# One PSUM tile for each accumulator, the inner values' sums moved to GpSimd and partly through DRAM, splits of 1024 columns on VectorE

## The chip, the cores and the metric

The kernel runs on one core of a Trainium2 chip. The metric is the device time of one execution in microseconds; the median of three runs is compared. The profile is of one further execution, so it has a time of its own.

## The reference

Three layers follow each other on 4608 tokens of 512 values:

```python
# attention in chunks of 64: 8 batches, 8 heads, 576 positions, head size 64
attn = softmax(q @ k.T / sqrt(64)); x = attn @ v          # x: (4608, 512) after heads are joined
# first layer: w_in (512, 2048), w_out (2048, 512)
h = x @ w_in
x = (h * clip(h + 3, 0, 6) / 6) @ w_out
# second layer: w_in2 (512, 1024), w_out2 (1024, 512), g_ln (1024)
h = x @ w_in2
solu = h * softmax(h)
out = ((solu - mean) / sqrt(var + 1e-6) * g_ln) @ w_out2
```

All is float32. Each factor of a product is split into a rounded part and a rest (`hi`, `lo`), and a product is three matmuls: hi x hi, lo x hi, hi x lo.

## The kernel before, in words

The tokens are nine blocks of 512 columns, and attention has 36 units of 128 tokens, four to a block. A manual order of instructions is written out: each engine runs its own in the order of the code. Every wait is put in by the framework between instructions that touch the same tile.

Blocks 0 to 2 run the first layer plainly (`moe_h`, `moe_gate`, `moe_split`, `moe_o`), one chunk of 128 of the 2048 hidden values at a time, with the attention of later blocks between them; during blocks 1 and 2 the kernel also forms sums of weights (`sums_of`, `split_sums`) and stores them in DRAM. The blocks 3 to 8 are done as three pairs. A pair is two blocks that are treated as a matrix of 2 x 2 parts, so that seven products do instead of eight; the seven factors on either side are sums such as S1, S2 of weights and T1, T2 of inputs. The first two pairs run `pair_7`, the last one `pair`, beside which the class `Second` prepares the weights of the second layer. Then the second layer runs to the end.

`pair_7` has two halves.

- First half: eight steps j over pairs of hidden chunks. A step has seven products `mul7` of six matmuls each into accumulators a, b and c. In order of TensorE: A11 into a (ScalarE copies it to s1); S2 into b (VectorE: u2 = s1 + b); S1 into c; then, in `finish`, the last two products of the step before, A22 into its b and S4 into its c; S3 into b (VectorE: u3 = s1 + b, c22 = u3 + c); A12 into a; at last `att_slot`, the scores of one attention unit and the product with v of another. Steps 0 and 5 have no unit. Each of the four hidden values (c11 from a, c21 from b, c12 and c22 from c) goes through the gate h * clip(h / 6 + 1/2, 0, 1). `ring_tile` gives the weights of a step two buffers each: wa (A11, A12, A22) and ws (S1 to S4); `fetch_next(j + 2, ...)` loads them, from the SP queue, when `finish` has used the old ones.
- Second half: seven products i of eight chunks j each (`mul_o`, six matmuls a chunk), whose inputs are sums of the gated values. `prepare` splits one chunk and then, for the first four products, forms in place the sum that a later product needs. Six chunks are prepared ahead. Steps of `prep(p + 1)` (the inputs of the next pair) and two attention units stand between.

In the first half a and b are the halves of one tile of two PSUM banks, `acc_psum(j % 2)`, and the four values go to SBUF tiles `g_t` before their gates, two of them with the product on GpSimd (`gate_there`, L1214). `moe_o` takes its four accumulators from the same two tiles. At the end of the second pair `load_o` (L1398) loads 16 tiles of 512 KB of weights for the last pair: 8 in the last product, 8 behind it. Scores of units from 20 on go through `attn_scores` (VectorE subtracts the maximum, one exponential on ScalarE, VectorE sums), those before through `attn_scores_act` (eight exponentials of one head each, with the maximum as bias and the sum as a second output).

A tile of 128 x 512 float32 is 256 KB, one of 128 x 2 x 512 is 512 KB.

Of the kernel before, what the change touches and what calls it, by code (L numbers as in the profile page):

```python
# [8 lines left out]
F32 = mybir.dt.float32  # L9
# [7 lines left out]
P = 128  # L17
# [4 lines left out]
def tile_kernel(  # L22
# [33 lines left out]
    held = nc.dram_tensor("held", (NF, P, BT), F32, kind="Internal").ap()  # L56

# [50 lines left out]
    ps_acc = es.enter_context(tc.tile_pool(name="ps_acc", bufs=1, space=PSUM))  # L108
# [580 lines left out]
    rescale("i", 2)  # L689
    x2, xr2 = {}, {}  # L690
# [293 lines left out]
    def att_slot(w, u):  # L984
# [15 lines left out]
    def soft(u):  # L1000
        if u in exps:
            attn_exp_act(u, range(H))
        attn_norm(u)
# [186 lines left out]
    N_C, AHEAD = len(OUTS) * NJ, 6  # L1190
# [14 lines left out]
    def gate(h, out):  # L1205
        t = gp.tile([P, BT], F32, tag="t", name="t")
        nc.scalar.activation(out=t, in_=h, func=AF.Relu, bias=half_1, scale=1.0 / 6.0)
        nc.vector.scalar_tensor_tensor(out=out, in0=t, scalar=1.0, in1=h, op0=ALU.min, op1=ALU.mult)

    def gate_there(h):  # L1210
        t = gp.tile([P, BT], F32, tag="t", name="t")
        nc.scalar.activation(out=t, in_=h, func=AF.Relu, bias=half_1, scale=-1.0 / 6.0)
        nc.scalar.activation(out=t, in_=t, func=AF.Relu, bias=one_1, scale=-1.0)  # L1213
        nc.gpsimd.tensor_mul(out=h, in0=t, in1=h)  # L1214

    def source(c):
        i, j = divmod(c, NJ)
        f, h = ((0, 0), (1, 1), (1, 0), (1, 1), (0, 0), (0, 1), (1, 0))[i]
        return g_t[2 * j + f][:, h]

    def entry(c):
        if c < 5 * NJ:
            return pair_of(wi_slot(4 + c % 10, F32R))
        k = c % 6
        if k < 4:
            return pair_of(wi_slot(10 + k, F32R))
        return [gp.tile([P, BT], F32R, tag=n, name=n) for n in ("g_hi", "g_lo")]
# [3 lines left out]
    def prepare(c):  # L1231
        if c >= N_C:
            return
        i, j = divmod(c, NJ)
        src = source(c)
        hi, lo = parts_o[c] = entry(c)
        nc.scalar.copy(out=hi, in_=src)  # L1237
        (nc.vector if j % 4 == 3 else nc.gpsimd).tensor_sub(out=lo, in0=src, in1=hi.bitcast(F32))  # L1238
        (b11, b12), (b21, b22) = (pair_of(g_t[2 * j + f]) for f in range(2))
        if i < 4:  # L1240
            o, x, y = ((b11, b12, b11), (b12, b22, b12), (b22, b22, b11), (b21, b21, b22))[i]
            nc.vector.tensor_sub(out=o, in0=x, in1=y)

    def mul_o(ps, i, j, start, stop):
        w, x = ring_o[i, j // (NJ // 2)][:, j % (NJ // 2)], parts_o.pop(i * NJ + j)
# [11 lines left out]
    def pair_7(p, todo):  # L1257
        b1, b2 = FIRST + 2 * p, FIRST + 2 * p + 1
        base = (b1 + 2) * UPB
        late = None  # L1260

        def finish(j, b, c, s1, u2):
            mul7(b, j, "A22", "T4", False, True)
            fetch_next(j + 2, 0)
            c21, c12 = g_t[2 * j + 1][:, 0], g_t[2 * j][:, 1]
            nc.vector.tensor_add(out=c21, in0=s1, in1=b)
            gate(c21, c21)
            mul7(c, j, "S4", "B22", False, True)
            fetch_next(j + 2, 1)
            nc.vector.tensor_add(out=c12, in0=u2, in1=c)  # L1270
            gate_there(c12)
            ring_w.pop(j)

        event = {1: 0, 2: 1, 3: 2, 4: 3, 6: 4, 7: 5}
        for j in range(NJ):
            u = base + event[j] if j in event else NU
            m = acc_psum(j % 2) if j else att_psum()
            a, b = m[:, 0], m[:, 1]
# [5 lines left out]
            if u < NU and u != NA:  # L1284
                soft(u)
# [3 lines left out]
            if u < NU and u != NA:  # L1289
                attn_turn(u, range(3))  # L1290
            c = h_psum()
            mul7(c, j, "S1", "T1", True, False)
            for f in range(2):
                g_t[2 * j + f] = wo_slot(2 * j + f, F32)
# [456 lines left out]
```

## Time and profile before

| | us |
|---|---|
| median of 3 runs | 1352.29 |
| lowest and highest | 1345.01, 1353.33 |
| profiled execution | 1355.62 |
| its span, first to last instruction | 1353.8 |

| engine | busy us | share of the span | instructions |
|---|---|---|---|
| TensorE, matmuls (PE) | 1211.1 | 89% | 7199 |
| TensorE, weight loads (PEld) | 975.7 | 72% | 7199 |
| VectorE (DVE) | 967.7 | 71% | 1474 |
| ScalarE (ACT) | 713.0 | 53% | 1481 |
| GpSimd (POOL) | 538.5 | 40% | 586 |

The mean granted clock of TensorE is 0.957. Matmuls are pipelined and a matmul's end is modelled, so the busy time of TensorE is longer than the time that its matmuls take from start to start. A share of the whole span is a mean over stages that have different limits; the stages have to be looked at one by one. SPq is the queue from which SyncE issues DMAs.

### The profile page before, as it was taken

To read this page: it belongs to the slowest core of one execution; us is meant where nothing else is said; L and a number is where in the kernel's file an instruction comes from. 1 tells how busy PE (TensorE), PEld (TensorE's weight loads), DVE (VectorE), ACT (ScalarE), POOL (GpSimd) and SP (SyncE) were. 2 spreads that over 40 slices of the span, in tenths; PEclk is the share of its full clock that TensorE was granted. 3 is DMA by queue.
4 is the path that set the end of the run, shared out by engine and by line. 5 is a ranking of instruction groups with operands and counts; after the bars stand their busy time and mean duration, and the time that the engine had idled before them with its cause. 6 is when DMAs were issued, how large, how long until landed. Compare 5 with 4: busy or idle time off the path is not lost. (4 is left out here: it accounts for less than half of the span.)

```text
span 1353.8 us, 20715 instructions
## 1 busy us (share of the span) xinstructions
PE 1211.1 (89%) x7199; PEld 975.7 (72%) x7199; DVE 967.7 (71%) x1474; ACT 713.0 (53%) x1481; POOL 538.5 (40%) x586
## 2 busy tenths in 40 slices
PE   8999979998778678977857967999999999999998
PEld 6888757786556457755645856888888888888887
DVE  7986656774655689665569854667698887877874
ACT  7874444543333424433343422435488777777775
POOL 1003553410311448511154731211037767667665
PEclk9999999999988879999887988999999999999999
DMA  9715789622553545544442689978522222222221
GB/s 374 288 48 192 284 310 323 207 71 76 177 176 132 179 140 171 187 156 156 143 172 90 219 296 347 346 288 317 191 94 91 70 93 92 69 92 93 71 76 62
DMA packets 131225, 235.49 MB, mean 174 GB/s; under 512 B 15408, under 2 KB 75056, under 8 KB 124464
## 3 DMA queue, kind: packets, MB, share of 16 engines
q1 hardware_dynamic: 125936, 224.72, 48.6%
q10 hardware_dynamic: 5184, 9.44, 1.8%
q8 instruction: 57, 0.93, 0.3%
q14 instruction: 48, 0.39, 0.1%
HBM read 157.81 MB, written 65.54 MB: 165 GB/s over the span
## 5 line engine op out<-in xcount | busy, mean ns | idle before, releaser
L573 PE MATMUL acc<-g_hi,wo 128*128 128x512 f32 x640 | 164.1, 396 | 0.8 <-ACT g_hi L556 0.5
L1214 POOL TENSOR_TENSOR wo<-t,wo 128x512 f32<-128x512 f32 x32 | 41.1, 1285 | 258.9 <-ACT t L1213 164.8
L1238 POOL TENSOR_TENSOR wi<-wo,wi 128x512 fp32r<-128x512 f32 x74 | 119.4, 1642 | 52.7 <-ACT wi L1237 51.9
L573 PEld LDWEIGHTS acc<-g_hi,wo 128*128 128x128 f32 x640 | 119.5, 189 | 27.4 <-DVE xo L586 1.1
L1112 PE MATMUL hp<-wi,ws 128*128 128x512 f32 x384 | 103.5, 411 | 9.5 <-DVE s L1425 9.5
L1112 PE MATMUL acc<-wi,wa 128*128 128x512 f32 x252 | 74.2, 435 | 40.7 <-DVE xo L1305 39.0
L855 ACT COPY wo<-wo 32x256 f32<-32x256 f32 x228 | 92.1, 404 | 19.6 <-DVE wo L837 11.6
L1112 PEld LDWEIGHTS hp<-wi,ws 128*128 128x128 f32 x384 | 77.7, 203 | 27.4 <-DVE s L1425 10.0
L534 PE MATMUL hp<-x_hi,wi 128*128 128x512 f32 x384 | 95.7, 391 | 0.1
L723 POOL TENSOR_TENSOR x_lo<-xr,x_hi 128x768 fp32r<-128x768 f32 (+1 forms) x30 | 63.4, 2134 | 75.1 <-ACT x_hi L716 75.1
L1112 PEld LDWEIGHTS acc<-wi,wa 128*128 128x128 f32 x252 | 49.2, 204 | 57.6 <-DVE xo L1305 44.9
L573 PE MATMUL acc<-g_lo,wo 128*128 128x512 f32 x320 | 87.6, 389 | 0.0
L534 PEld LDWEIGHTS hp<-x_hi,wi 128*128 128x128 f32 x384 | 71.6, 188 | 15.4 <-ACT x_hi L511 0.3
L1237 ACT CAST wi<-wo 128x512 fp32r<-128x512 f32 x100 | 56.1, 622 | 37.2 <-PE hp L1248 25.0
L827 DVE SCALAR_TENSOR_TENSOR wo<-wo,r,wo 128x1024 f32<-128x1024 f32 x36 | 70.3, 1954 | 1.3
L1112 PE MATMUL acc<-wi,ws 128*128 128x512 f32 x168 | 47.9, 424 | 24.0 <-ACT s L1281 19.8
L573 PEld LDWEIGHTS acc<-g_lo,wo 128*128 128x128 f32 x320 | 60.1, 188 | 12.7
L559 POOL TENSOR_TENSOR g_lo<-t,g_hi 128x512 fp32r<-128x512 f32 x15 | 21.4, 1425 | 118.3 <-ACT g_hi L556 114.9
L924 POOL TENSOR_TENSOR wo<-wo,wo 128x1024 fp32r<-128x1024 f32 x25 | 63.2, 2527 | 6.5 <-ACT wo L920 3.5
L1112 PEld LDWEIGHTS acc<-wi,ws 128*128 128x128 f32 x168 | 32.3, 199 | 36.2 <-ACT s L1281 25.0
L540 ACT ACTIVATE t<-hp,three 128x512 f32<-128x512 f32 x48 | 33.3, 694 | 46.3 <-PE hp L534 46.3
L1248 PE MATMUL acc<-wi,ws 128*128 128x512 f32 x192 | 47.6, 396 | 10.1 <-DVE wi L1238 8.2
(331 smaller groups left out, 3148.1 us busy)
## 6 DMA issues: line engine op xcount, KB each, us to landing
ws<-sts SPq DMA_DIRECT2D x24, 1024.0 KB, 7.0
wa<-sto SPq DMA_DIRECT2D x14, 1024.0 KB, 4.9
ws<-sto SPq DMA_DIRECT2D x14, 1024.0 KB, 6.0
wa<-stw SPq DMA_DIRECT2D x24, 512.0 KB, 3.4
wo<-wo SPq DMA_DIRECT2D x328, 32.0 KB, 1.8
x2d<-xo SPq DMA_DIRECT2D x36, 256.0 KB, 4.1
xr<-x2d SPq DMA_DIRECT2D x36, 256.0 KB, 3.6
out<-ob SPq DMA_DIRECT2D x36, 256.0 KB, 2.3
```

The lines of the kernel that those rows point to most:

```text
L534: nc.tensor.matmul(hp, wi[f][:, a, kk * P : (kk + 1) * P], b[:, kk], start=(n == 0), stop=(n == 3 * KD - 1),)
L540: nc.scalar.activation(out=t, in_=hp, func=AF.Relu, bias=three[:])
L573: nc.tensor.matmul(acc[dc], wo[f][:, w, dc * P : (dc + 1) * P], g[i], start=(at == 0 and n == 0), stop=(at == NF - 1 and n == 2),)
L723: eng.tensor_sub(out=lo[:, f], in0=r, in1=hi[:, f].bitcast(F32))
L827: nc.vector.scalar_tensor_tensor(out=h, in0=e, scalar=r, in1=h, op0=ALU.mult, op1=ALU.mult, accum_out=mu)
L855: move(out=m[b * 32 : b * 32 + 32, a], in_=tr[a * 32 : a * 32 + 32, b])
L924: eng.tensor_sub(out=lo, in0=m, in1=hi.bitcast(F32))
L1112: nc.tensor.matmul(ps, w[:, i, kk * P : (kk + 1) * P], x[:, kk], start=(start and n == 0), stop=(stop and n == 5), skip_group_check=True,)
L1214: nc.gpsimd.tensor_mul(out=h, in0=t, in1=h)
L1237: nc.scalar.copy(out=hi, in_=src)
L1238: (nc.vector if j % 4 == 3 else nc.gpsimd).tensor_sub(out=lo, in0=src, in1=hi.bitcast(F32))
L1248: nc.tensor.matmul(ps[s], w[:, k, s * P : (s + 1) * P], x[l], start=(start and j == 0 and n == 0), stop=(stop and j == NJ - 1 and n == 2), ...
```

## The change

- `moe_o` and `pair_7` take each accumulator from a tile of its own, one bank (`acc_bank`). In `pair_7` step j uses banks 0 and 1 or 2 and 3 by turns.
- The four values stay in PSUM: the sums of `finish` are written back into b and c, ScalarE makes the ramp of the gate (`ramp`) and VectorE multiplies from PSUM (`gate`). Only c22 still has its product on GpSimd.
- The sums that the second half needs are formed in the first half on GpSimd (`later_sums`, four for each step). T1 stays in SBUF; T2, T3 and T4 are written to the DRAM tensor `later_t` from `xo` tiles, and `bring` loads them in the first three products of the second half over values that are used up.
- `prepare` splits two chunks at once: one copy of 1024 columns on ScalarE, one subtraction of 1024 on VectorE. Three double chunks are prepared ahead. For each third one of the last two products it splits two times 512.
- In the first half the scaling of a unit by its sums runs on GpSimd (`soft(u, nc.gpsimd)`); all scores go through `attn_scores_act`.
- `load_o` is issued one tile at a time from the third product of the second pair's second half on. The last unit of `sums_of("o", ...)` moves from the first pair to block 2. The steps of `prep` lie at other places.

```diff
-                acc[2 * i], acc[2 * i + 1] = pair_of(acc_psum(i))
+                acc[2 * i], acc[2 * i + 1] = acc_bank(2 * i), acc_bank(2 * i + 1)
...
+    es_acc.close()
+    ps_bank = es.enter_context(
+        tc.tile_pool(name="ps_bank", bufs=1, space=PSUM, reuse_waits="tile")
+    )
+
+    def acc_bank(i):
+        return ps_bank.tile([P, DM], F32, tag=f"b{i}", name=f"acc{i}")
...
-            (attn_scores_act if u < (FIRST + 2) * UPB else attn_scores)(u, sc)
+            attn_scores_act(u, sc)
...
-        if u in exps:
-            attn_exp_act(u, range(H))
-        attn_norm(u)
+        attn_exp_act(u, range(H))
+        attn_norm(u, eng)
...
+    GROUPS = ("B11", "T1", "B22", "B21")
+    HOMES = ("B11", "B22", "B21", "B11", "T1", "B22", "B21")
...
+        i, m = divmod(d, ND)
+        src = g_t[HOMES[i], m]
+        e = entry(d)
...
+            nc.scalar.copy(out=e[0], in_=src)
+            nc.vector.tensor_sub(out=e[1], in0=src, in1=e[0].bitcast(F32))
+            e = [pair_of(t) for t in e]
...
+    def bring(d):
+        i, m = divmod(d, ND)
+        if 0 <= i < 3:
+            t = g_t[HOMES[i], m] = home(HOMES[i], m)
+            nc.sync.dma_start(out=t, in_=later_t[i, m])
...
+            nc.vector.tensor_add(out=b, in0=s1, in1=b)
+            t = gp_tile("t")
+            ramp(b, t)
             mul7(c, j, "S4", "B22", False, True)
             fetch_next(j + 2, 1)
+            nc.vector.tensor_add(out=c, in0=u2, in1=c)
+            gate(t, b, g_t["B21", j // 2][:, j % 2])
+            t = gp_tile("g_hi")
+            ramp(c, t)
             ring_w.pop(j)
+            while waiting:
+                waiting.pop(0)()
+            return j, t, c
+
+        def later_sums(j, g12):
+            m, k = j // 2, j % 2
+            g11, g22, g21, t1 = (g_t[n, m][:, k] for n in ("B11", "B22", "B21", "T1"))
+            t2, t3, t4 = (work_tile("xo") for _ in range(3))
+            sub = nc.gpsimd.tensor_sub
+            sub(out=t1, in0=g12, in1=g11)
+            sub(out=t2, in0=g22, in1=t1)
+            sub(out=t3, in0=t2, in1=g11)
+            sub(out=t4, in0=g21, in1=t2)
+            for i, t in enumerate((t2, t3, t4)):
+                waiting.append(
+                    lambda i=i, t=t: nc.sync.dma_start(out=later_t[i, m][:, k], in_=t)
+                )
...
-            m = acc_psum(j % 2) if j else att_psum()
-            a, b = m[:, 0], m[:, 1]
+            n = 2 * ((j + 1) % 2)
+            old = p == 0 and j == 0
+            a = att_psum()[:, 0] if old else acc_bank(n)
...
+                soft(u, nc.gpsimd)
+            b = h_psum() if old else acc_bank(n + 1)
...
+            if made:
+                i, t, ps = made
+                gate(t, ps, t)
+                later_sums(i, t)
             mul7(b, j, "S3", "T3", False, False)
-            u3 = work_tile("xo")
+            u3 = ap1.tile([P, DM], F32, tag="tx2", name="tx2")
...
+        for d in range(2):
+            prepare(d)
+        i, t, ps = finish(*late)
+        gate(t, ps, t)
+        prepare(2)
+        later_sums(i, t)
...
+        steps = (
+            (2, 1), (2, 5), (3, 1), (3, 5), (4, 2), (4, 4), (4, 5), (5, 1), (5, 5), (6, 5)
+        )
...
+                if (i, j) == (0, 5):
+                    while waiting:
+                        waiting.pop(0)()
+                if j % 2:
+                    bring(d)
+                else:
+                    prepare(d + 3)
...
+                    f = d + 2 - 3 * ND
+                    if j % 2 and 0 <= f < NF:
+                        load_o(f)
...
-        if p == NPAIR - 2:
-            for f in range(8, NF):
-                load_o(f)
...
-    UNITS |= {2 * j: ("o", j - 5) for j in range(NJ, NJ + 4)}
+    UNITS |= {2 * j: ("o", j - 5) for j in range(NJ, NJ + 5)}
```

## Rows read from the trace of the kernel before

**Rows 1.** Busy time by stage: stretch, length, engines, granted clock, DMA share, GB/s.
```profile
280.00:313.00 33.00, 33.00 (x205) 27.21 (x204) 22.23 (x34) 12.43 (x23) 0.54 (x1) 1.00 0.15 49
...
315.70:460.60 144.90, 106.48 (x745) 80.49 (x745) 78.65 (x126) 50.86 (x85) 29.18 (x24) 0.89 0.45 150
460.60:565.10 104.50, 87.97 (x465) 69.70 (x464) 89.59 (x88) 42.26 (x75) 68.32 (x42) 0.90 0.52 173
565.10:694.40 129.30, 96.53 (x721) 72.79 (x721) 75.62 (x126) 46.25 (x76) 23.37 (x18) 0.91 0.46 152
694.40:794.30 99.90, 85.45 (x433) 68.22 (x432) 86.82 (x88) 42.94 (x76) 68.23 (x42) 0.93 0.53 177
794.30:837.80 43.50, 26.48 (x97) 20.50 (x96) 17.23 (x28) 9.08 (x15) 2.59 (x2) 0.84 0.98 340
837.80:1001.00 163.20, 163.14 (x706) 134.31 (x707) 115.25 (x182) 78.59 (x133) 23.76 (x21) 0.98 0.73 263
...
1001.00:1353.00 352.00, 348.99 (x1540) 288.66 (x1538) 274.93 (x416) 264.91 (x492) 236.17 (x335) 1.00 0.27 84
```

**Rows 2.** Waits, whole span: waiter, released by, us in total, times, longest.
```profile
PE acc L1112 <- DVE xo L1305: 39.0, 14, 10.0
PE acc L1112 <- ACT s L1281: 19.8, 12, 2.8
```

**Rows 3.** Timeline of TensorE, steps 1 and 2 of the first pair.
```profile
348.58 0.69 PE L397 MATMUL att<-kbd,q 64*64 64x64 f32 x32
...
349.67 1.66 PE L1112 MATMUL acc<-wi,wa 128*128 128x512 f32 x6
...
357.47 1.52 PE L1112 MATMUL hp<-wi,ws 128*128 128x512 f32 x6
358.83 1.52 PE L1112 MATMUL acc<-wi,ws 128*128 128x512 f32 x6
362.20 2.56 PE L1112 MATMUL acc<-wi,wa 128*128 128x512 f32 x6 [1.84 <-DVE xo L1305]
```

**Rows 4.** DMA issues in the two first halves: size, median us to landing.
```profile
ws<-sts SPq DMA_DIRECT2D x7, 1024.0 KB, 7.0
wa<-stw SPq DMA_DIRECT2D x7, 512.0 KB, 3.2
...
x2d<-xo SPq DMA_DIRECT2D x3, 256.0 KB, 6.4
```

**Rows 5.** VectorE by line: min, median, max ns.
```profile
L811 DVE TENSOR_TENSOR wo<-u,c x16: 689/689/689, 1016.8 to 1322.8; 128x512 f32<-128x512 f32 x16
...
L453 DVE TENSOR_SCALAR sm<-sm x35: 158/172/1124, 9.7 to 727.3; 128x8 f32<-128x8 f32 x34, 128x16 f32<-128x16 f32 x1
...
L493 DVE STREAM_TRANSPOSE pbd<-p x116: 432/436/440, 99.6 to 734.7; 32x256 f32<-32x256 f32 x116
```

**Rows 6.** Timeline of ScalarE: first and last exponential of a unit.
```profile
40.42 0.30 ACT L447 ACTIVATE p<-att,mx 128x64 f32<-128x64 f32 x1
...
42.45 0.35 ACT L447 ACTIVATE p<-att,mx 128x64 f32<-128x64 f32 x1
```

**Rows 7.** GpSimd by line: min, median, max ns.
```profile
L1214 POOL TENSOR_TENSOR wo<-t,wo x32: 1265/1287/1302, 333.2 to 697.8; 128x512 f32<-128x512 f32 x32
...
L464 POOL TENSOR_TENSOR p<-p,sm x2: 1042/1042/1043, 10.3 to 12.5; 128x512 f32<-128x512 f32 x2
```

**Rows 8.** VectorE by line, both operands in SBUF: min, median, max ns.
```profile
L1242 DVE TENSOR_TENSOR wo<-wo x32: 677/1774/1787, 447.0 to 754.1; 128x512 f32<-128x512 f32 x32
...
L1129 DVE TENSOR_TENSOR wi<-wi,wi x6: 1210/1225/2308, 530.1 to 809.1; 128x1024 fp32r<-128x1024 f32 x6
```

**Rows 9.** What ended TensorE's idle time before the second halves' matmuls (L1248).
```profile
  DVE wi L1238: 21.0, 10
```

**Rows 10.** Timeline of the passage to the last pair.
```profile
806.02 0.43 DVE L257 TENSOR_SCALAR q<-xr 128x512 int32<-128x512 int32 x1 [8.99 <-DMA xr<-in_moe_w_in]
...
808.12 2.93 PE L1112 MATMUL hp<-wi,ws 128*128 128x512 f32 x6 [9.54 <-DVE s L1425]
```

More of the change, by code (lines that the diff above doesn't have):

```diff
@@ L1216, in source, with ramp @@
[L1216 to L1227, printed above, removed]
+    def ramp(h, t, down=False):
+        s = -1.0 / 6.0 if down else 1.0 / 6.0
+        nc.scalar.activation(out=t, in_=h, func=AF.Relu, bias=half_1, scale=s)
+        if down:
+            nc.scalar.activation(out=t, in_=t, func=AF.Relu, bias=one_1, scale=-1.0)
@@ new lines, in gate, with gp_tile, home, entry @@
+    def gate(t, h, out):
+        nc.vector.scalar_tensor_tensor(out=out, in0=t, scalar=1.0, in1=h, op0=ALU.min, op1=ALU.mult)
+    def gp_tile(tag, dtype=F32):
+        return gp.tile([P, BT], dtype, tag=tag, name=tag)
+    GROUPS = ("B11", "T1", "B22", "B21")
+    HOMES = ("B11", "B22", "B21", "B11", "T1", "B22", "B21")
+    ND = NJ // 2
+    def home(name, m):
+        return wo_slot(GROUPS.index(name) * ND + m, F32)
+    def entry(d):
+        if d < 5 * ND:
+            return [wi_slot(4 + 2 * (d % 5) + i, F32R) for i in range(2)]
+        k = d % 3
+        if k < 2:
+            return [wi_slot(10 + 2 * k + i, F32R) for i in range(2)]
+        return None
@@ L1259, in pair_7 @@
         base = (b1 + 2) * UPB
-        late = None
+        late, made, waiting = None, None, []
         def finish(j, b, c, s1, u2):
@@ L1288, in pair_7 @@
             nc.vector.tensor_add(out=u2, in0=s1, in1=b)
[L1289 to L1290 removed]
+            if j % 2 == 0:
+                for g in GROUPS:
+                    g_t[g, j // 2] = home(g, j // 2)
+            m, k = j // 2, j % 2
+            if late and late[0] == 0:
+                made = finish(*late)
             c = h_psum()
             mul7(c, j, "S1", "T1", True, False)
[L1293 to L1294 removed]
             o_next()
[L1296 to L1302 removed]
+            if late and late[0] > 0:
+                made = finish(*late)
+            if u < NU and u != NA:
+                attn_turn(u)
+            if made:
+                i, t, ps = made
+                gate(t, ps, t)
+                later_sums(i, t)
             mul7(b, j, "S3", "T3", False, False)
[L1304 removed]
+            u3 = ap1.tile([P, DM], F32, tag="tx2", name="tx2")
             nc.vector.tensor_add(out=u3, in0=s1, in1=b)
[L1306 removed]
+            c22 = g_t["B22", m][:, k]
             nc.vector.tensor_add(out=c22, in0=u3, in1=c)
[L1308 removed]
+            t = gp_tile("g_lo")
+            ramp(c22, t, True)
+            nc.gpsimd.tensor_mul(out=c22, in0=t, in1=c22)
             mul7(a, j, "A12", "B21", False, True)
[L1310 removed]
+            t = gp_tile("t")
+            ramp(a, t)
             o_next()
@@ L1313, in pair_7 @@
                 att_slot(u, u + 1)
-            if p == 0 and j == 1:
-                sums_of("o", NJ - 1)
-            elif p == 0 and j == 2:
-                for i in range(2):
-                    split_sums("o", NJ - 1, i)
-            late = j, b, c, s1, u2
-        finish(*late)
-        for n in range(3, AHEAD):
-            prepare(n)
+            gate(t, a, g_t["B11", m][:, k])
+            late = j, b, c, s1, u2
+        for d in range(2):
[4 more added lines that the diff above has]
+        later_sums(i, t)
         s1 = [work_tile("s") for _ in range(2)]
         m3 = [work_tile("s") for _ in range(2)]
-        u2 = [gp.tile([P, BT], F32, tag="t", name="u2") for _ in range(2)]
+        u2 = [gp_tile("t") for _ in range(2)]
         todo = prep(p + 1)
-        steps = {(2, 5): 1, (3, 1): 1, (3, 3): 1, (3, 5): 1, (5, 0): 1, (5, 2): 1, (5, 3): 1, (5, 5): 1, (5, 7): 1, (6, 5): 1}
+        steps = (
+            (2, 1), (2, 5), (3, 1), (3, 5), (4, 2), (4, 4), (4, 5), (5, 1), (5, 5), (6, 5)
+        )
+        final = p == NPAIR - 2
         a = b = c = None
@@ L1331, in pair_7 @@
             if i in (0, 6):
-                a = pair_of(acc_psum(0))
+                a = [acc_bank(n) for n in range(2)]
             elif i == 1:
@@ L1335, in pair_7 @@
             elif i == 3:
-                b = pair_of(acc_psum(1))
+                b = [acc_bank(n) for n in range(2, 4)]
             ps = (a, c, a, b, c, b, a)[i]
@@ L1383, in pair_7 @@
             if i == 5:
-                c22 = []
                 for s in range(2):
@@ L1388, in pair_7 @@
                     store_x(b2, 2 + s, xo)
-        if p == NPAIR - 2:
-            for f in range(8, NF):
-                load_o(f)
         return todo
```

64 lines of the change are left out of this document (20 added, 44 removed).

## The prediction, made before the change was timed

> **What bounds the kernel now.** The busy time by stage comes first [rows 1]. The stretch from 315.7 to 794.3 us is the two pairs that `pair_7` does, each as a first half (hidden layer, `mul7`) and a second half (`mul_o`); 43.5 us of passage into the last pair follow, and then that pair. The reader is to see two things. The last pair runs the same kind of products with TensorE busy 163.14 of 163.20 us; in the four halves no engine is full: in the first one TensorE is busy 106.48 of 144.90 us, VectorE 78.65, ScalarE 50.86, GpSimd 29.18, DMA 0.45, and the granted clock is 0.89 to 0.93 where the last pair has 0.98. So nothing is short of capacity there; TensorE waits for single results. The window just before the first pair (280 to 313) has TensorE busy throughout.
>
> Next the timeline of TensorE [rows 3], for the price without waits: a group of six matmuls (one call of `mul7`) starts 1.36 us before the next one (357.47 to 358.83), 0.227 a matmul; an attention unit is 348.58 to 349.67, 1.09. Each half has 336 matmuls: 76.2 us. With the 24 `moe_o` matmuls left over (5.4) and six units (6.5) the first half of the first pair has 88.1 us of work in 144.9, of the second 82.7 in 129.3; the second halves 78.4 in 104.5 and about 77.8 in 99.9; the passage 97 matmuls, 22.0 in 43.5. That is 172 us to be had, and no more.
>
> Then what ended the waits [rows 2]: TensorE on `acc` waited 39.0 us for u3 = s1 + b (L1305) and 19.8 for the copy of a (L1281). That is 2.8 and 1.65 each time. The timeline shows one: A12 begins 3.37 us after S3 (358.83, 362.20), where 1.36 would do; the other stands between A11 and S2. S2 writes b and has nothing to do with the copy of a; A12 writes a and has nothing to do with the sum that reads b. They wait because a and b are the two halves of one PSUM tile. In the last pair they are tiles of their own, and there is no such wait.
>
> **Part 1, a tile for each accumulator.** Both false waits go; they cost about 2 us each a step, plus the slow matmuls behind a gap. What is late next has to be found, since the step can't fall below 7 x 1.36 + 1.09 = 10.6 us. I see three circles.
> (a) Weights. `ring_tile` has two buffers, so the load of S weights for step j+2 is issued after S4 of step j, in step j+1, and lands 7.0 us later [rows 4]; S2 of j+2 needs it. From S2 to S4 the step has the four groups S2, S1, A22, S4: 5.44 + 7.0 = 12.4 us a step. The A weights have more room: 5.44 + 3.2 for the larger transfer.
> (b) VectorE. Nine ops of 0.69 (u2, u3, c22, two `finish` sums, three gates, the maximum), a full transpose taken at 0.69 also, four small ones of 0.436, three ops of 0.17 (epsilon, reciprocal, scaling of the maximum) [rows 5]: 9.1. All scores now go through `attn_scores_act`: eight exponentials with their sums on ScalarE, 40.42 to 42.80, 2.4 us [rows 6], and VectorE's next instruction (epsilon) waits for them with the whole queue behind it. 11.5, near 12 with the handovers.
> (c) GpSimd. Four sums and one product of 1.287 and the scaling of a unit, 1.042 where it ran on GpSimd [rows 7]: 7.5 us a step, so it has room. But the sums write into the four `xo` tiles, three a step, and two of them wait until the stores of the step before have landed. A store took 6.4 us [rows 4]; then two sums 2.6, product 1.3, scaling 1.0, transposes 2.4, unit 1.1, and five groups 6.8 to the next store: 21.6 for two steps, 10.8 each. If the store first stands behind the S weights (about 9 us), 12.1.
> I take the largest, 12.4, and 0.4 for their interplay: 12.8. Both ends are kept: 10.6 (all hidden) and 15 (the circles add up in part).
> First pair: step 0 has five groups and two `moe_o` (6.8 + 5.4) and about 1.6 for the two splits ahead of u2; seven steps of 12.8; `finish` 2.7: 106 instead of 144.9. Second: 8.3 + 89.6 + 2.7 = 101 instead of 129.3. Together -67.
>
> **Part 2, sums on GpSimd in the first half.** It runs beside VectorE, so the price of company counts. A VectorE op with two operands in SBUF takes 0.677 alone and mostly 1.774 beside GpSimd (L1242) [rows 8]; one with an operand in PSUM stays at 0.689 (L811) [rows 5], in a stage where GpSimd is busy for 236 of 352 us [rows 1]. In the new first half nearly every VectorE op reads a PSUM tile, since the sums stay in b and c. So I charge nothing there, and find the exception at the seam: the first three 1024-column splits have both operands in SBUF and run beside the last sums, up to 2.308 instead of 1.225 [rows 8].
> Epsilon's row has a median of 0.172 and a maximum of 1.124 [rows 5], so some of these tiny ops do wait. The Trainium skill, SBUF — State Buffer, Who interferes with whom, says that `tensor_scalar` can take the port pair it shares with GpSimd and that the second to issue blocks until the first is done. By that, with GpSimd busy in over half of a step, two such ops would wait some 0.4 us each (an estimate), 10 us over the two pairs, and the time would be 1260; the row's median is against it, its maximum for it.
> The transfers: three stores of 256 KB a step and twelve loads of 512 KB, 6.3 MB each way in each pair. In a first half 150 GB/s x 144.9 us = 21.7 MB become 28 MB in 106: 264 GB/s; the passage moved 340 [rows 1]. Hidden, but (c) hangs on it.
>
> **Part 3, splits of 1024 columns on VectorE.** The second half loses its time to splits [rows 9]: 21.0 us for VectorE's. Removed from each: 32 sums on VectorE (many at 1.774) and 56 splits of 512 columns, 42 of them on GpSimd. Added: 28 splits of 1024 at 1.225, 34 us. With ten steps of `prep` (12.5), outputs (8) and two units (8) VectorE has 63 us in 78. Left are the start, where the last gates, two to three splits beside GpSimd and a unit's scaling and transposes come together (about 7 us late by 3 x 1.1 and 3.5 of scaling and transposes in one product's 10.9 us), and the second unit, some 3: 90 instead of 104.5, -14. If the seam is covered, -24; if it isn't at all, 0.
>
> **Part 4, `load_o` earlier.** The passage waits for DMA at share 0.98: VectorE stood 8.99 us for a raw weight of the second layer, and TensorE 9.54 behind it [rows 10]. The sixteen loads (8.4 MB) now begin in the fourth product of the second pair's second half, spread over its rest. The bytes don't go: 177 x 99.9 + 340 x 43.5 = 32.5 MB, and 6.3 of the detour, 38.8 MB, 114 us at 340 GB/s. TensorE has 78 + 22 and the 10 of part 3. I take 120 for 143.4, -23; bounds 112 and 135.
>
> **The rest.** The one unit of `sums_of("o", 7)` moves from the first pair to the blocks at F = 24 to 26 (two VectorE ops of 0.69, four GpSimd ops, eight small stores on SP's queue). There TensorE is full and VectorE two thirds busy (22.23 of 33.00) [rows 1]; I take nothing, and 2 us if that cover fails. `soft` at F = 27 gets the exponentials: 2.4 us of a ScalarE that is busy for 12.43 of those 33. For `moe_o`, bank by bank instead of pair by pair, under 1 us.
>
> Sum: -67 - 14 - 23 = -104. The profiled execution took 1355.6, 3.3 above the median of 1352.3, so 1248; I say 1250.
>
> **Rivals.** A: all three circles are hidden, and the first halves run at TensorE's pace: 14 steps of 2.2 us less, 1219. For it: the last pair does it; against it: that pair loads its weights a whole step ahead and has no attention. B: the circles add up, since VectorE's queue waits for GpSimd's scaling, GpSimd for stores, and stores for VectorE's gates: 15 us a step and half of part 3 lost, +31 and +12: 1293. For it: a wait at the head of an in-order queue passes to all that stands behind it, and each circle crosses VectorE's. C: the false waits aren't that, but true ones; then only parts 3 and 4 are left, 1315. Against it: what the two instructions read and write. D: slower than before. The stores land late: the circle in (c) is (15.2 + landing) / 2, and reaches the old step of some 17 us (144.9 less about 20 for step 0 and `finish`, over seven) if a store takes 19 us from its issue. At 25 us a step takes 20, 14 steps lose 42, parts 3 and 4 return 20 of their 37, as their transfers slow as well: 1374. It decides from 19 us; the stores here took 6.4, and DMA is at 0.8 of what it moved in the passage.
>
> **Chances.** Forecast 0.58, A 0.14, B 0.22, C 0.03, D 0.03. The range reaches to A and B and takes the bounds of parts 3 and 4 on the better side only half, since they would have to come on top of A: 1215 to 1298. A measurement tells a change from none at about 1%, 13 us. Faster 0.95, same 0.02, slower 0.03.
>
> **What would show it.** Right: no wait of TensorE for L1305's or L1281's successor; steps of 12 to 13.5 us, S2 released by the DMA of S weights or the unit by transposes; VectorE's ops on PSUM at 0.69 though GpSimd is over half busy; second halves near 90 us with no wait for sums; the passage without a 9 us hole. Wrong: GpSimd waiting for the stores with units late behind it (B, D), S2 waiting for u3 or a copy (C), weights landing later than 9 us, or VectorE's splits at 2.3 throughout.

## The result, and the profile after

The changed kernel takes 1262.56 us (median of four runs, 1260.79 to 1264.40) against 1352.68 (four runs) for the kernel before: a ratio of 0.9346, 95% interval 0.9309 to 0.9383. Forecast was 1250, range 1215 to 1298. The profiled execution took 1264.4 us, its span is 1262.5, the mean granted clock 0.977.

First the same view as [rows 1], of the changed kernel: first half, second half, first half, second half, passage, and the first 163.2 us behind the passage.

```profile
core 0: us, PE busy (x) PEld busy (x) DVE busy (x) ACT busy (x) POOL busy (x), PEclk, DMA share, GB/s
316.20:434.60 118.40, 98.59 (x745) 76.62 (x743) 66.75 (x118) 51.55 (x148) 47.75 (x39) 0.96 0.65 215
434.60:520.90 86.30, 81.51 (x464) 66.56 (x465) 66.57 (x77) 43.09 (x81) 14.40 (x9) 0.96 0.82 306
520.90:631.40 110.50, 94.36 (x722) 73.36 (x721) 67.04 (x118) 50.26 (x157) 50.30 (x41) 0.94 0.68 222
631.40:717.60 86.20, 81.78 (x432) 66.40 (x433) 64.09 (x74) 41.73 (x80) 12.10 (x8) 0.94 0.96 363
717.60:749.80 32.20, 24.74 (x98) 19.70 (x97) 21.74 (x34) 12.34 (x19) 2.91 (x3) 0.84 0.88 323
749.80:913.00 163.20, 163.20 (x721) 135.10 (x720) 115.56 (x181) 80.70 (x137) 24.47 (x22) 1.00 0.72 257
```

The last window has the length of the one in [rows 1] because it was cut so; it doesn't end at the same matmul. From the first group behind the passage to the first matmul of the second layer what is left of the last pair takes 163.8 us before (837.86 to 1001.67) and 160.5 after (749.81 to 910.31); what follows takes 352.1 and 352.2. So all but 3 us of the difference lies ahead of the last pair:

| stage | before | forecast | after |
|---|---|---|---|
| first half, pair 1 | 144.9 | 106 | 118.4 |
| second half, pair 1 | 104.5 | 90 | 86.3 |
| first half, pair 2 | 129.3 | 101 | 110.5 |
| second half of pair 2 and passage | 143.4 | 120 | 118.4 |

The first halves gained 45.3 us and not 67; the rest gained 43.2 and not 37. The granted clock of the first halves rose from 0.89 and 0.91 to 0.96 and 0.94.

Next, what TensorE waits for, as in [rows 2], over the whole span.

```profile
PE acc L1121 <- DMA ws<-sts: 17.9, 7, 4.0
...
PE hp L1121 <- DVE s L1479: 7.5, 1, 7.5
PE acc L1270 <- DVE wo L1220: 7.2, 2, 3.8
PE acc L1121 <- DVE s L1331: 6.5, 5, 2.0
```

The two false waits of [rows 2], 58.8 us in all, are gone: neither the copy of a nor u3 heads a wait of this size. In their place S2 waits for S weights (17.9 us, seven times; five of them in pair 1) and S3 for u2 (L1331; 1.5 to 2.0 us in three steps of pair 2). In the circle of VectorE stands an instruction that waits itself. Here is the timeline in a step of pair 1 and one of pair 2; the bracket is the idle time before the instruction and what ended it.

```profile
358.13 1.83 PE L1121 MATMUL acc<-wi,ws 128*128 128x512 f32 x6 [2.14 <-DMA ws<-sts]
358.36 0.69 DVE L411 TENSOR_REDUCE mx<-att 128x8 f32<-128x512 f32 x1 [2.66 <-ACT wi L521]
359.10 1.30 POOL L1308 TENSOR_TENSOR xo<-xo,wo 128x512 f32<-128x512 f32 x1 [2.00 <-DMA later_t<-xo]
...
541.64 0.72 ACT L1215 ACTIVATE g_lo<-wo,three 128x512 f32<-128x512 f32 x1 [4.65 <-DVE wo L1353]
542.39 0.72 ACT L1217 ACTIVATE g_lo<-g_lo,three 128x512 f32<-128x512 f32 x1
543.02 0.67 ACT L1215 ACTIVATE t<-acc,three 128x512 f32<-128x512 f32 x1
543.59 0.36 ACT L521 COPY xr<-att 128x256 f32<-128x256 f32 x1
543.84 0.38 ACT L521 COPY wi<-att 128x256 f32<-128x256 f32 x1
544.26 0.69 DVE L411 TENSOR_REDUCE mx<-att 128x8 f32<-128x512 f32 x1 [2.66 <-ACT wi L521]
...
548.23 0.17 DVE L455 TENSOR_SCALAR sm<-sm 128x8 f32<-128x8 f32 x1 [1.96 <-ACT p L449]
548.56 0.63 DVE L1331 TENSOR_TENSOR s<-s,acc 128x512 f32<-128x512 f32 x1
549.25 1.81 PE L1121 MATMUL acc<-wi,ws 128*128 128x512 f32 x6 [1.90 <-DVE s L1331]
```

The maximum of a unit's scores (L411) reads the PSUM tile from which ScalarE copies another unit's result (L521), and those copies stand in ScalarE's queue behind two ramps for c22 and one for a. One `att` tile holds the scores of one unit and the result of another, and VectorE waits 2.66 us, with everything behind it. Over the span this is `DVE mx L411 <- ACT wi L521`, 34.2 us, 15 times. Then epsilon (L455) waits 1.96 us for the exponentials, u2 comes after that, and S3, which writes b, waits for u2.

### The profile page after: what moved, and what is told of

It is laid out like the page before. It is cut to its first block, busy times and chain, and to the rows that moved or that the text cites. A ratio compares the mean times of both kernels' runs of the same rounds, so it can differ in the third digit from the quotient of the medians.

```text
span 1262.5 us, 20959 instructions
## 1 busy us (share of the span) xinstructions
PE 1186.9 (94%) x7199; PEld 965.6 (76%) x7199; DVE 900.8 (71%) x1433; ACT 721.8 (57%) x1655; POOL 478.3 (38%) x561
## 4 chain that ended last, share of the span: by engine, by line
PE 73%; DVE 7%; DMA 7%; ACT 4%; POOL 4%; issue 4%; SPq 2%; POOLq 0%; ACTq 0%
PE po L950 16%; PE acc L575 13%; PE acc L1270 9%; PE hp L536 6%; PE hp L1121 6%; PE b L752 5%; PE hp L1270 3%; PE a L752 3%; PE c L752 3%; PE acc L1121 2%; PE att L1121 2%; DMA ws<-sts 2%; POOL xo L1070 2%; ACT p L449 1%; DMA later_t<-xo 1%
## 5 line engine op out<-in xcount | busy, mean ns | idle before, releaser
L449 ACT ACTIVATE p<-att,mx 128x64 f32<-128x64 f32 x256 | 76.7, 325 | 22.9 <-DVE mx L432 22.9
L1255 DVE TENSOR_TENSOR wi<-wo,wi 128x1024 fp32r<-128x1024 f32 x50 | 67.4, 1368 | 24.8 <-ACT wi L1254 23.2
L1121 PE MATMUL acc<-wi,wa 128*128 128x512 f32 x270 | 73.3, 410 | 1.3 <-DVE tx L1351 1.3
L1121 PE MATMUL acc<-wi,ws 128*128 128x512 f32 x180 | 51.2, 423 | 24.5 <-DMA ws<-sts 17.9
L1254 ACT CAST wi<-wo 128x1024 fp32r<-128x1024 f32 x50 | 51.6, 1071 | 34.1 <-PE acc L1270 16.4
L575 PEld LDWEIGHTS acc<-g_lo,wo 128*128 128x128 f32 x320 | 60.4, 189 | 12.9
L1270 PE MATMUL acc<-wi,wa 128*128 128x512 f32 x216 | 57.0, 419 | 12.5 <-DVE wo L1220 7.2
L1121 PEld LDWEIGHTS acc<-wi,wa 128*128 128x128 f32 x270 | 52.4, 198 | 13.6 <-DVE tx L1351 1.5
L1270 PEld LDWEIGHTS acc<-wi,wa 128*128 128x128 f32 x216 | 43.4, 204 | 24.4 <-DVE wo L1220 8.0
```

The costliest lines, as they stand in the source:

```text
L449: nc.scalar.activation(out=p_t[u][:, h], in_=sc[:, c, a], func=AF.Exp, scale=0.125, bias=mx[:, m : m + 1], accum_out=sums[u][:, h : h + 1],)
L575: nc.tensor.matmul(acc[dc], wo[f][:, w, dc * P : (dc + 1) * P], g[i], start=(at == 0 and n == 0), stop=(at == NF - 1 and n == 2),)
L1121: nc.tensor.matmul(ps, w[:, i, kk * P : (kk + 1) * P], x[:, kk], start=(start and n == 0), stop=(stop and n == 5), skip_group_check=True,)
L1255: nc.vector.tensor_sub(out=e[1], in0=src, in1=e[0].bitcast(F32))
L1270: nc.tensor.matmul(ps[s], w[:, k, s * P : (s + 1) * P], x[l], start=(start and j == 0 and n == 0), stop=(stop and j == NJ - 1 and n == 2), ...
```

## The experiments

Each kernel was timed in three or more rounds beside the kernel before. Stage lengths are taken from the first matmul of a stage to the first of the next, the rest from the passage to the last instruction of the profiled execution.

**What the parts are worth.** The changed kernel with accumulators 2i and 2i+1 as halves of one tile:

```diff
+    both = {}
...
     def acc_bank(i):
-    return ps_bank.tile([P, DM], F32, tag=f"b{i}", name=f"acc{i}")
+    if i % 2 == 0:
+        both[i] = ps_bank.tile([P, 2, DM], F32, tag=f"b{i}", name=f"acc{i}")
+    return both[i - i % 2][:, i % 2]
```

> Edit to the changed kernel: part 1 undone alone; accumulators 2i and 2i + 1 are again the two halves of one PSUM tile, everything else stays. Theory (false waits between a and b cost 2 to 4.5 us a step): S2 waits for the copy of a and A12 for u3 again, 14 steps, partly beside the wait for weights: 1295 to 1325 us. Rival (the gain came from the other parts; the rival C of the prediction): within 10 us of 1262.6.

1300.24 us, ratio 0.9609 (0.9575 to 0.9643): 38 us lost, and the wait for u3 is back, here of the kernel with shared tiles:

```profile
PE acc L1125 <- DVE tx L1355: 44.8, 15, 3.8
...
PE acc L1125 <- ACT s L1327: 8.8, 13, 0.7
```

The opposite, the kernel before with part 1 alone:

```diff
...
-            m = acc_psum(j % 2) if j else att_psum()
-            a, b = m[:, 0], m[:, 1]
+            n = 2 * ((j + 1) % 2)
+            old = p == 0 and j == 0
+            a = att_psum()[:, 0] if old else acc_bank(n)
...
+            b = h_psum() if old else acc_bank(n + 1)
...
```

> The kernel before with part 1 alone: each accumulator in a tile of its own, the sums, gates and splits where they were; step 1 of each pair does the last products of step 0 ahead of S1, as the changed kernel does. If the parts add up, this gains what the changed kernel loses when its accumulators share tiles, 38 us: 1312 to 1318. If the false waits are all that the first halves lost (58.8 us), 1292 to 1300. If the tiles help only once the sums are out of the way, 1325 to 1345.

1313.27 us, 0.9707 (0.9655 to 0.9760): 37.3 us below the kernel before in the same runs. The two together place each part:

| kernel | first halves | second halves |
|---|---|---|
| before | 144.9, 129.3 | 104.5, 99.9 |
| before, part 1 alone | 118.9, 113.8 | 104.6, 100.5 |
| after, tiles shared | 142.1, 135.8 | 79.6, 78.4 |
| after | 118.4, 110.5 | 86.3, 86.2 |

Part 1 alone brings nearly the whole gain of the first halves: without the other parts they take 118.9 and 113.8 already. But they are held there by another wait, TensorE's largest in the kernel before with part 1 alone (whole span):

```profile
PE att L398 <- DVE pbd L494: 44.4, 16, 8.6
```

It is the wait for a unit's transposes on VectorE; 25.7 us of it lie in the first halves, 17.1 of them at the last unit of either. In the changed kernel it is 4.1 there, and the wait for S weights is 17.9 instead of 11.5. So the halves are equally long in part for different reasons, and what the other parts would be worth in the first halves without the late weights these runs do not show. The second halves owe their gain to the sums and splits; part 1 adds nothing there. Moving the sums to GpSimd costs the first halves next to nothing (142.1 and 135.8 with shared tiles against 144.9 and 129.3). With shared tiles the first halves are so slow that the first splits of the second half are covered (two are done by 453.5, its first matmul starts at 456.75), and it runs at 79.6 and 78.4, where TensorE is busy all the time:

```profile
456.80:536.40 79.60, 78.96 (x465) 65.07 (x466) 58.40 (x71) 41.20 (x79) 8.65 (x6) 1.00 0.86 320
...
672.20:750.60 78.40, 78.40 (x432) 64.59 (x433) 56.42 (x68) 40.17 (x78) 9.19 (x6) 1.00 1.02 389
```

**The width of the splits.** 56 subtractions of 512 columns in place of 28 of 1024 (the loop over `src[:, k]`):

> The changed kernel, but VectorE splits each double chunk with two subtractions of 512 columns instead of one of 1024; ScalarE's copies stay at 1024. If the width is what part 3 gives, as VectorE fills the second half (81.8 of 86.3 us of TensorE's rhythm), 56 subtractions of 0.68 in place of 28 of 1.23 add 3.6 us to each second half: 1268 to 1271. If what counts is that the sums and the products of GpSimd are gone from the second half, the width is worth nothing: 1260 to 1265.

1261.94 us, 0.9322 (0.9263 to 0.9382): no difference in time. Its second halves are 88.4 and 87.1, 2.9 us longer together; its first halves happen to be shorter by 4.4. So the width is worth 3 us at most. That leaves for part 3 the removal of the sums and of GpSimd's splits, which no run takes one by one.

**The loads for the last pair at their old place:**

```diff
...
-                    f = d + 2 - 3 * ND
-                    if j % 2 and 0 <= f < NF:
-                        load_o(f)
+                    if i == 6 and j % 2:
+                        for f in (j - 1, j):
+                            load_o(f)
...
+        if p == NPAIR - 2:
+            for f in range(8, NF):
+                load_o(f)
...
```

> Edit to the changed kernel: part 4 undone alone; the 16 loads for the last pair stand again in the last product and behind it. Theory: the passage takes 43 us again instead of 32, and the second half of the second pair stays at 86: 1270 to 1278 us. Rival (the passage shrank because the rest of the queue was relieved): within 3 us of 1262.6.

1272.74 us, 0.9410 (0.9380 to 0.9440): part 4 is worth 10 us, and it lies in the passage, 42.4 us here against 32.2:

```profile
712.60:755.00 42.40, 27.65 (x100) 21.51 (x99) 16.46 (x28) 9.62 (x15) 2.57 (x2) 0.84 1.00 350
```

**Why the first halves fell short.** Four runs alter the order in a step, and two leave out the detour through DRAM. First `att_slot` with its copies ahead of the ramps:

```diff
+            mul7(a, j, "A12", "B21", False, True)
+            o_next()
+            if u < NU:
+                att_slot(u, u + 1)
             t = gp_tile("g_lo")
             ramp(c22, t, True)
             nc.gpsimd.tensor_mul(out=c22, in0=t, in1=c22)
-            mul7(a, j, "A12", "B21", False, True)
             t = gp_tile("t")
             ramp(a, t)
-            o_next()
-            if u < NU:
-                att_slot(u, u + 1)
```

> Edit: in a step of the first half ScalarE copies the attention unit before it makes the ramps of c22 and a; nothing else. Theory V (VectorE's circle holds the step: its maximum of the next unit stands 2.7 us behind ScalarE's copies, so the circle is 11.5 + 2.7 = 14.2 us): the maximum's waits for the copies, 34.2 us, fall below 10, S3 no longer waits for u2, and the steps fall to what the weights allow, some 13.3: 8 steps by about 1 us, 1250 to 1256 us. Theory W (the weights' circle alone holds the step): the waits for the maximum go as well, but the time stays within 3 us of the changed kernel's 1262.6.

1253.11 us, 0.9268 (0.9240 to 0.9297). The maximum's waits for L521 fall from 34.2 us to 3.7, S3's for u2 from 6.5 to 1.2, and the first halves are 111.8 and 108.7. What is left is the weights:

```profile
PE acc L1121 <- DMA ws<-sts: 22.4, 10, 4.6
```

Then, on the changed kernel, the S weights released earlier, S4 ahead of A22 in `finish` (the sum and the ramp of c go with S4):

```diff
+            mul7(c, j, "S4", "B22", False, True)
+            fetch_next(j + 2, 1)
...
             mul7(b, j, "A22", "T4", False, True)
             fetch_next(j + 2, 0)
...
-            mul7(c, j, "S4", "B22", False, True)
-            fetch_next(j + 2, 1)
...
```

> Edit: finish runs S4 into c before A22 into b, so that the S weights are loaded one product earlier and in front of the A weights. Theory W: S2's 17.9 us of waits for the S weights go nearly all, with the slow matmuls behind them: 1244 to 1252 us. Theory V: the steps stay near 14.2, the wait moves from S2 to S3 (u2): no more than 4 us faster, 1258 to 1264.

1270.93 us, 0.9392 (0.9376 to 0.9408): slower by 8 us, a miss. And both together:

> Edit: those two together. If both circles stand side by side (V and W each true of some steps), only this frees the steps: attention steps of 12 to 12.8 us as predicted, 14 steps by 1.5 us less, 1236 to 1246 us. If one alone binds, it is no faster than the better one of the two runs before it.

1270.97 us, 0.9386 (0.9363 to 0.9409), a miss too. The S weights land sooner, but the A weights, issued behind them, land later (6.4 us, after: 3.4), and A11 comes ahead of S2. The DMA issues in the two first halves and the wait, of the kernel with S4 first:

```profile
ws<-sts SPq DMA_DIRECT2D x15, 1024.0 KB, 4.8
wa<-stw SPq DMA_DIRECT2D x15, 512.0 KB, 6.4
...
PE acc L1121 <- DMA wa<-stw: 13.9, 7, 4.7
```

Next, on the changed kernel, the detour left out: no store to `later_t` and no load from it, so T2, T3 and T4 of the second halves are left-over values.

```diff
-            t = g_t[HOMES[i], m] = home(HOMES[i], m)
-            nc.sync.dma_start(out=t, in_=later_t[i, m])
+            pass
...
-                    lambda i=i, t=t: nc.sync.dma_start(out=later_t[i, m][:, k], in_=t)
+                    lambda: None
```

> Edit: the 48 stores to later_t and the 24 loads from it are left out; the sums are still formed, but the second halves read what lay in the tiles before (T2, T3 and T4 are wrong, all instructions of the engines stay). Prices the detour through DRAM. Theory W: the S weights land again 7.0 us after their issue instead of 7.9, GpSimd's 21.7 us of waits for stores go, and the steps with a wait of S2 lose nearly 1 us each: 1250 to 1256. Theory V: the time stays within 3 us, as these waits lie beside VectorE's circle.

1253.08 us, 0.9264 (0.9248 to 0.9281). The S weights land in 7.1 us and their wait falls from 17.9 to 9.8. Of the 9.5 us, 7.0 lie in the first halves (112.7 and 109.2) and 2.5 in the second halves (85.2 and 84.8):

```profile
PE acc L1121 <- DVE s L1330: 9.9, 8, 2.0
PE acc L1121 <- DMA ws<-sts: 9.8, 5, 3.8
```

Last, the products of the step before right after A11, on top of the copies:

```diff
-            if u < NU and u != NA:
-                soft(u, nc.gpsimd)
+            unit = u < NU and u != NA
+            if unit:
+                attn_exp_act(u, range(H))
+            if late:
+                made = finish(*late)
+            if unit:
+                attn_norm(u, nc.gpsimd)
...
-            if late and late[0] == 0:
-                made = finish(*late)
...
-            if late and late[0] > 0:
-                made = finish(*late)
...
```

> Edit, on top of the copies-first kernel (1253.1): finish, with A22 and S4 of the step before, runs right behind A11 instead of behind S1, so that from S4 to the S2 that needs the next S weights there are seven products and a unit (10.6 us) instead of three and a unit. Theory W (what is left in the first halves is the wait for S weights, 22.4 us and the slow matmuls behind it): those waits go, steps of 11 to 12 us, 1224 to 1236 us. Rival V2 (VectorE's circle of 12 to 13 us, or GpSimd's waits for stores, 29.8 us, is next at once): 1238 to 1250, with the wait at S3 or at the unit.

1230.53 us, 0.9096 (0.9069 to 0.9124), the fastest kernel of the study. No wait for S weights is left, though they land in 7.3 us: S4 now stands ahead of S2 in a step, so the circle from S4 to S2 and on to the next S4 spans two steps, (7.3 + 10.6) / 2 = 9.0 us each, and no longer sets the pace. Its first halves, and its largest wait on `acc`:

```profile
316.60:416.50 99.90, 92.20 (x745) 72.44 (x743) 66.95 (x117) 49.82 (x148) 49.04 (x40) 1.00 0.78 256
...
503.50:598.50 95.00, 86.42 (x721) 67.99 (x719) 65.90 (x117) 48.46 (x157) 50.33 (x41) 1.00 0.78 255
...
PE acc L1121 <- DVE s L1336: 12.3, 12, 1.3
```

The time is as theory W had it, but what is left is named in V2: S3 waits for u2 in twelve steps, up to 1.3 us each, so VectorE's circle sets the pace, 12.4 us from one S3 to the next in steps with a unit.

The same version without the detour:

> The version with both reorderings (unit's copies ahead of the ramps, products of the step before right after A11), and without the 48 stores and 24 loads of the detour; T2, T3 and T4 of the second half are then left-over values, so the output is not the reference's. In the changed kernel the detour cost 9.5 us by way of late weights. If that was its only cost, it is free now, as TensorE no longer waits for weights in the first halves: 1226 to 1231. If the stores still cost through GpSimd's waits for them or through the passage's loads: 1218 to 1224.

1229.27 us, 0.9086 (0.9037 to 0.9134), first halves 99.9 and 94.6: within the intervals the detour costs nothing once the S weights have room. So what it cost in the first halves was late weights; for the 2.5 us of the second halves this is not shown.

**Two waits that only moved.** The passage with another order of the preparation for the second layer (in step 0 of the last pair `fill.window(1, 0)` left to the next call, `window(2, 2)` after u2):

> Edit, on top of that: in step 0 of the last pair VectorE forms u2 before it takes up the raw weight of the second layer. Theory: the 7.5 us hole of the passage is VectorE's wait for that weight at the head of its queue: the hole falls to 1 to 3 us, 4 to 6 us faster than the run before it. Rival: the passage is bound by DMA (share 0.88) and the wait only moves to u3 or to a later product: within 2 us.

1231.95 us, 0.9104 (0.9081 to 0.9128): no gain, as the rival said; that DMA is what binds is not shown. TensorE's hole moves by one group and grows, 7.00 us (released by L1480) in the version without it, here 7.97 behind a copy of the prepared weight:

```profile
692.96 0.67 ACT L156 ACTIVATE xr<-xr 128x512 f32<-128x512 f32 x1 [3.63 <-DMA xr<-in_moe_w_in]
...
700.16 2.90 PE L1121 MATMUL hp<-wi,wa 128*128 128x512 f32 x6 [7.97 <-ACT wi L320]
```

And the seam: the second half's accumulators in the banks that the last step does not hold, and three double chunks split ahead of the last gates.

```diff
-            n = 2 * ((j + 1) % 2)
+            n = 2 * ((j + p + 1) % 2)
...
-        for d in range(2):
+        for d in range(3):
             prepare(d)
         i, t, ps = finish(*late)
         gate(t, ps, t)
-        prepare(2)
...
-                a = [acc_bank(n) for n in range(2)]
+                a = [acc_bank(2 * ((p + 1) % 2) + n) for n in range(2)]
...
-                b = [acc_bank(n) for n in range(2, 4)]
+                b = [acc_bank(2 * (p % 2) + n) for n in range(2)]
```

> The version with both reorderings, in which the second half takes the two banks that the last step of the first half does not hold (the pairs alternate), and the third double chunk is split ahead of the last products' gates. In the first product of the second half TensorE stood 3.76 us behind the gate of the bank that it takes (twice, 7.5 us in all). If that reuse of banks is the price of the seam, the wait for the gate is gone and the time falls by 5 to 9 us, to 1221 to 1226. If the splits beside GpSimd, 2.0 us each, set the pace there anyway, the waits only pass to them: 1228 to 1232.

1235.84 us, 0.9141 (0.9120 to 0.9162): 5.3 slower than without it, outside both expectations. The wait for the gate is gone, and the first four of the eight chunks of the first product (24 matmuls) take 8.6 us (415.25 to 423.85) instead of 13.6, but the unit that follows now waits for its transposes:

```profile
423.85 5.60 PE L1270 MATMUL acc<-wi,ws 128*128 128x512 f32 x24
...
433.75 0.33 PE L399 MATMUL att<-pbd,v 64*64 64x64 f32 x4 [3.68 <-DVE pbd L495]
```

The 5 us come back there with more (second halves 89.7 and 88.6, where the version without it has 87.0 and 85.9): it seems that what VectorE and ScalarE have to do at the seam stays, and this order only chooses who waits for it.

## Why the prediction held, and where it did not

**The sign, the place and the rank of the parts** were right. The false waits were the largest loss, and the last pair and the second layer stayed as they were but for 3 us. Rival C (true waits) is excluded by part 1 alone: 37.3 us. Rival D did not come: the stores land in 8.5 us, not 19. Rival A, circles hidden at 1219, was not reached even by the best order. Rival B was right in part: circles did add up, as the maximum joins ScalarE's queue to VectorE's, but in the first halves only.

**First halves: the step of 12.8 us was sized too small.** It measured 11.5 to 18.5 in pair 1, from A11 to A11, a mean of 14.5 over steps 2 to 7: 6 x 1.7 = 10 of the 12.4 us that this half fell short. Two terms failed, and each set the pace of steps of its own.

Circle (b), VectorE's, was put at 11.5 to 12 and has the 2.7 us of L411 in it as well, 14.2. It holds pair 2: in three steps on end S3 waits for u2 and starts 14.2 us after the one before (549.25, 563.44, 577.64). I counted what VectorE does and the exponentials it waits for, and not that its maximum shares a PSUM tile with copies at the end of ScalarE's queue. That resembles the error that I had just diagnosed for a and b, with one difference: a and b lay in two banks of their tile, while scores and result have 256 columns each of the same two banks (`part_of`). Whether VectorE waits because of the tile or because of the banks no run separates.

Circle (a), the weights', holds pair 1, where S2 waits for S weights in every step from 3 on. It was put at 12.4 and measured 13.6 to 16.6, from one issue of S weights to the next (349.91, 365.53, 379.60, 393.21, 409.79). It had the landing of [rows 4], 7.0 us; the stores of 256 KB in the same half raise it to 7.8 (7.1 without them), and S2 starts 7.8 to 8.3 us after the issue. From there to the next issue it had 5.44; that took 5.8 where the granted clock stayed at 1.00, and 7.4 and 8.6 in the two steps in which it was 0.71 (358.1 to 363.9) and 0.57 (401.2 to 408.2) behind the wait, stretches with time at both levels, 1.2 and 2.4 GHz. I had named slow matmuls behind a gap, but for the old waits and not in this circle. The slow stretches, and the missing unit of step 5, are why single steps differ so much. Why the clock fell behind waits of 2.14 and 3.99 us and stayed behind 2.21, 1.76 and 1.92 is open.

With (b) mended (copies ahead of the ramps), S weights are issued every 13.8, 13.5, 13.1 and 15.3 us in pair 1. Why this circle gets shorter too is seen only in part: the clock falls once (0.78 from 395.1 to 402.3) instead of twice. With (a) mended as well (products right after A11), steps with a unit take 11.5 to 12.9 from step 2 on, the clock of the first halves stays at 1.00, and VectorE's circle is at 12.4, near the 12 of the prediction.

The DMA issues of the changed kernel in the two first halves:

```profile
ws<-sts SPq DMA_DIRECT2D x15, 1024.0 KB, 7.8
later_t<-xo SPq DMA_DIRECT2D x45, 256.0 KB, 8.5
wa<-stw SPq DMA_DIRECT2D x14, 512.0 KB, 3.4
```

Circle (c) was not the limit. GpSimd does wait for the stores (`POOL xo L1308 <- DMA later_t<-xo`, 21.7 us in nine waits), but no TensorE wait hangs on it: without the detour and with early S weights the first halves are the same.

**Part 2, no charge for GpSimd's company,** was right for the ops that read PSUM. From 316 to 632 us, by line of VectorE, min, median and max ns (the sums of `finish`, and the scaling of the maximum):

```profile
L1287 DVE TENSOR_TENSOR acc<-s,acc x14: 683/689/697, 348.9 to 619.4; 128x512 f32<-128x512 f32 x14
...
L432 DVE TENSOR_SCALAR mx<-mx x14: 170/398/1287, 345.3 to 629.5; 128x8 f32<-128x8 f32 x14
```

The 0.689 of [rows 5] holds, although GpSimd is busy for 40 to 46% of the half, less than the "over half" that I wrote. But the tiny ops on SBUF do pay. Here are the scaling of the maximum (L432) and epsilon (L455), busy us and mean ns over the same stretch, and one scaling beside GpSimd:

```profile
L432 DVE TENSOR_SCALAR mx<-mx 128x8 f32<-128x8 f32 x14 | 7.0, 501 | 0.5
L455 DVE TENSOR_SCALAR sm<-sm 128x8 f32<-128x8 f32 x13 | 6.6, 511 | 23.5 <-ACT p L449 23.5
...
544.37 1.29 POOL L1309 TENSOR_TENSOR xo<-wo,xo 128x512 f32<-128x512 f32 x1
544.99 0.70 DVE L432 TENSOR_SCALAR mx<-mx 128x8 f32<-128x8 f32 x1
```

The 27 ops took 13.6 us; at 0.17 each it would be 4.6. Fifteen of them did take 0.17. The other twelve are those that began more than 0.01 us into a GpSimd operation, and each ended 0.02 to 0.04 us after that operation did (here 545.69 and 545.66). By the Trainium skill, SBUF — State Buffer, Who interferes with whom, an op of VectorE with at most one operand from SBUF keeps clear of GpSimd outside the modes that take two ports, while `tensor_scalar` can enter such a mode and then be blocked for the whole of GpSimd's instruction; the trace agrees with the first (0.689) and with the second. So the 10 us that I worked out by that rule and set aside are nearly there, 9.0 us of VectorE's time: I judged by the median, 0.172 for epsilon here too, where the sum counts. How much of the 9 us reached the time no run shows. That the rule's 1260 lies near the measured 1262.6 is chance, as the first halves fell short by 22 us for the terms above.

**Second halves and the seam** were right in size and place. Forecast was -14 with 7 us lost at the start and -24 if the seam is covered; measured were -18.2 and -13.7, 86.3 and 86.2 long, and -24.9 and -21.5 where slow first halves cover it (shared tiles). The first four of the eight chunks of the first product take 12.76 us (434.67 to 447.43) instead of 5.44. The seam of pair 1:

```profile
434.49 4.00 DVE L1255 TENSOR_TENSOR wi<-wo,wi 128x1024 fp32r<-128x1024 f32 x2
434.67 0.70 PE L1270 MATMUL acc<-wi,wa 128*128 128x512 f32 x2 [1.96 <-ACT wi L1254]
435.16 2.25 POOL L1309 TENSOR_TENSOR xo<-wo,xo 128x512 f32<-128x512 f32 x1
...
440.59 7.00 PE L1270 MATMUL acc<-wi,wa 128*128 128x512 f32 x21 [3.76 <-DVE wo L1220]
```

The splits take 2.0 us each beside GpSimd, as [rows 8] had it. What I did not see is that the matmul at 440.59 waits for a gate: the second half takes the two banks that the last step still holds. The 3 us for the second unit did not show.

**Part 4** was right in sum (118.4 for 120) and wrong in one sign of it. I expected a passage without a 9 us hole; one of 7.46 us is left, behind the raw weight of the second layer as in [rows 10]. The later holes are gone instead (two of 2.99 and 4.40 us in the kernel with the loads at their old place).

```profile
727.25 0.43 DVE L259 TENSOR_SCALAR q<-xr 128x512 int32<-128x512 int32 x1 [4.47 <-DMA xr<-in_moe_w_in]
729.36 2.93 PE L1121 MATMUL hp<-wi,ws 128*128 128x512 f32 x6 [7.46 <-DVE s L1479]
```

**The rest** was put at nothing and gave 3 us: from the passage's end to the end of the span 512.7 us against 515.9. All of it lies at the head of the last pair, and it is the clock. In the kernel before, TensorE stands 5.24 us at the passage's end (released by L1434), and the next three groups start 2.72, 2.56 and 1.76 us apart instead of 1.36. The first 7.2 us behind the passage, before and after:

```profile
837.80:845.00 7.20, 7.14 (x19) 5.63 (x20) 4.80 (x9) 1.90 (x3) 1.62 (x1) 0.57 1.00 401
...
749.80:757.00 7.20, 7.20 (x33) 5.98 (x32) 3.68 (x6) 3.63 (x7) 2.61 (x2) 1.00 0.75 273
```

A granted clock of 0.57 is nearly all the lower level, 1.2 GHz. In the changed kernel the hole is gone and the clock is 1.00 there, 2.4 GHz. With the loads at their old place a hole of 4.40 us is back, the clock behind it is 0.62 (754.4 to 758.9), and the same groups take 1.8 us longer; so at least that much belongs to part 4.

**The sum.** -45 instead of -67, -43 instead of -37 and -3 instead of nothing make -92 for -104; the medians differ by 90. The mechanisms that the prediction names were at work, but the maximum's wait for the copies was not among them, and the first halves were mis-sized by 22 us. That 9 of these came back in other stages was not foreseen; it is luck.

## What to carry to other kernels

When a false wait between two users of one tile is found, look for every other tile with two users before sizing what comes next; here undoing the second wait gave 9.5 us, where the time lay 12.6 above the forecast. A circle through DMA is the landing plus the work between use and release, and moving the release across the use (S4 ahead of S2) doubles its room, while swapping two releases only hands the wait to the other transfer. Where several results are late at once, as at the seam and in the passage, removing the wait that the trace names may only move it. For the price of company take the sum over all instances of an op, not its median: a few long ones can hide behind many short ones. And cut windows that are to be compared at the same instructions, not at the same length.

## What was not expected of the hardware

The S weights and A weights of a step share the queue: issued first, the 1 MB of S weights lands in 4.8 us and the 512 KB behind it in 6.4; issued second, it lands in 7.8 and the 512 KB in 3.4. The order of two issues moves 3 us from one to the other. In the second half of pair 2 with shared tiles DMA moved 389 GB/s over 78.4 us, where the passage before, at share 0.98, moved 340 [rows 1]; so that was no ceiling, though I divided by it.
